# Pairs of kv tiles summed by accumulating transfers ahead of the pooling matmuls

## The chip, the cores and the metric

The kernel runs on one core of a Trainium2 chip. The metric is the device time of one execution in microseconds (us); lower is better. The median of three runs of the kernel before is 1297.57 us (1297.37 to 1297.65).

## The reference, cut to what matters

Three stages follow each other. Attention with keys and values that are pooled 4 x 4 and projected, then a gated MLP (GELU by sigmoid), then a second gated MLP (hard swish):

```python
kv_pool = kv.reshape(B, H // 4, 4, W // 4, 4, C).mean(axis=(2, 4))
k = v = kv_pool.reshape(B, -1, C) @ w_sr            # 768 keys, C = 128
a = softmax(q @ k.T / sqrt(C))                      # q: 12288 rows
x = a @ v
h = x @ moe_w_in;  x = (h * sigmoid(1.702 * h)) @ moe_w_out        # d_ff = 2048
h = x @ moe2_w_in; x = (h * clip(h + 3, 0, 6) / 6) @ moe2_w_out
```

Everything is float32. The change is in the first two lines: how the sixteen elements of each pooling window come to be summed.

## The kernel before, in words

**Tiles.** The launch code lays kv out as 3 groups of 256 keys by 4 tiles. A kv tile (`kvs`) is 128 channels by 1024 columns, 512 KB: four window elements of the 256 keys of a group. Twelve tiles come in by twelve plain loads on SyncE's queue (L578), in the order of the string `LOADS`, in which `k` is the next kv tile, `w` a 512 KB weight block (raw 64-bit words, L210) and `q` the first q tile (256 KB, L178).

**Pooling by TensorE.** `pool_mm(i)` (L590) multiplies tile i by `w_sr` in four matmuls of 256 columns, all accumulating into one PSUM tile of the group, so that the matmul does the projection and the sum of the window at once. The profile lists each float32 matmul of the program as two records. Before the first of them, `WARM` matmuls on the identity run (L561). The end of a group frees `k_hi` (L602, ScalarE), `k_lo` (L607, VectorE) and `k_copy` (L614); the last group's k is what the first score matmuls (L291) wait for.

**The head.** The string `HEAD` writes out, by hand, the order of everything up to the first two finished attention tiles: `K.i` pools tile i, `kh.g`, `kl.g`, `kf.g`, `V.g` make keys and values of group g, `Q` splits a q tile, `S`, `M`, `E`, `N` are scores, maximum, exponential and norm, `T`, `H`, `L` turn the exponentials round, `A`, `X` multiply by the values. `w.a`, `w.m`, `w.b`, `w.c`, `w.h`, `w.d` are the six steps by which VectorE and ScalarE turn one raw weight block into two float32 parts (L232 to L262). An engine takes its own instructions in this order; what stands for different engines in between matters only by the waits.

**After the head** come units of the MLPs: unit s writes 2 x 128 hidden rows (`unit_mm`), and three units later its output matmuls. `ORDER` gives the order of the pieces beside a unit, `W_STEPS` in which unit the remaining weight steps run, `T_STEPS_0` and `NORM_STEPS` where the third and fourth attention tile are turned and normed.

**Queues.** SyncE's queue issues loads in program order. A transfer that takes the place of one eight transfers back (the one load on ScalarE's queue counted in) waits until that one has landed, so that issue times tell landing times.

Of the kernel before, what the change touches and what calls it, by code (L numbers as in the profile page):

```python
# [11 lines left out]
F32 = mybir.dt.float32  # L12
# [3 lines left out]
ALU = mybir.AluOpType  # L16
AX = mybir.AxisListType

P = 128
# [18 lines left out]
H_STEPS = (6, 7, 8), (14, 16, 17)  # L38
AV_STEPS = (10, 10), (18, 18)
S_STEPS = (16, 18, 20, 22), (24, 26, 28, 30)  # L40
NORM_STEPS = 12, 12
T_STEPS_0 = {2: (3, 5, 8, 11), 3: (15, 17, 19, 21)}
V_STEPS_0 = {4: (40, 41, 42, 43), 5: (51, 51, 52, 52)}
D_STEPS_0 = {4: 44, 5: 53}
H_STEPS_0 = {4: (48, 49, 50), 5: (58, 59, 60)}
# [5 lines left out]
POOL_LO = 49, 51, 53, 57, 59  # L51

ORDER = {
    0: "v t_hi h_hi gelu t_lo w_hi w_hi_0 d hi w_0 rest hi_last h_lo w lo lo_last end".split(),
    1: "t_hi t_lo gelu hi_last hi h_hi lo_last lo v h_lo d end rest".split(),
    2: "table max w_hi_0 relu swish hi_last exp h_hi w_hi w_0 lo_last norm v h_lo d end rest w".split(),
    3: "hi_last relu lo_last swish end".split(),
}


LOADS = "k k k k w k k w k k k w k k q k w w"
HEAD = (
# [9 lines left out]
).split()  # L72


WARM = 10
W_SLOTS = 0, 1, 2, 3, 4, 3, 4, 3, 3
W_NEXT = 0, 0, 0, 1, 1, 1, 0, 1, 1, 1, 1, 0
D_POOL = (8, 11)
W_POOL = ()
W_STEPS = (  # L80
# [5 lines left out]
)  # L86
TOGETHER = 1

# [6 lines left out]
def tile_pooled_attention__moe_gelu__moe_hardswish(  # L95
# [16 lines left out]
    nc = tc.nc  # L112
    C, N = qT.shape
# [11 lines left out]
    ps_acc = ctx.enter_context(tc.tile_pool(name="ps_acc", bufs=2, space=bass.MemoryType.PSUM))  # L125
# [3 lines left out]
    ident = tiny.tile([P, P + 48], F32, name="ident", bufs=1)[:, :P]  # L129
# [3 lines left out]
    v_h = const.tile([P, KC, C], F32R, name="v_h")  # L133
    v_l = const.tile([P, KC, C], F32R, name="v_l")
# [21 lines left out]
    def f(ap):  # L156
        return ap.bitcast(F32)
# [4 lines left out]
    def act_hi(hi, x):  # L162
        nc.scalar.activation(hi, x, AF.Copy)  # L163

    def dve_lo(lo, x, hi):
        nc.vector.tensor_tensor(out=lo, in0=x, in1=f(hi), op=ALU.subtract)  # L166
# [102 lines left out]
    h = NK // 2  # L269
# [183 lines left out]

    for t, steps in T_STEPS_0.items():
        for i, step in enumerate(steps):
            at(step, "first", t_mm, t, i)
            at(step, "t_hi", t_hi, t, i)
            at(step, "t_lo", t_lo, t, i)
    for k, step in enumerate(NORM_STEPS):
        at(step, "rest", s_norm, FOUR - 1, 2 * k + 1, 2)  # L460
# [6 lines left out]
    for k in range(FOUR, NT, 2):  # L467
        s0 = 2 * k * NU
        for i in range(2):
            if k + 2 + i < NT:  # L470
                v, hh, av = ([s0 + x for x in y[i]] for y in (V_STEPS, H_STEPS, AV_STEPS))
# [84 lines left out]
    with tc.manual_schedule():  # L556
        make_identity(nc, ident)
        nc.scalar.dma_start(out=wsr_sb, in_=w_sr)
        warm = big()
        for _ in range(WARM):  # L560
            nc.tensor.matmul(warm[:, 0, :P], ident, ident, start=True, stop=True)  # L561

        n_g, n_w, kw = kvT.shape[1:]
        kg = NK // n_g
        banks = [("h", 2), ("h", 2), ("st", 1)]
        kvs, pk, kf = [], {}, {}
        for i in range(n_g * n_w):
            if i in (0, 3):
                kv3 = work.tile([P, 3, kw], F32, tag="eTl" if i else "eTh", name="kvs", bufs=1)
            if i < 6:  # L570
                kvs.append(kv3[:, i % 3, :])
            else:
                kvs.append(work.tile([P, kw], F32, tag="gl" if i % 2 else "gh", name="kvs", bufs=3))
        kv = 0
        for what in LOADS.split():
            if what == "k":
                g, w = divmod(kv, n_w)
                nc.sync.dma_start(out=kvs[kv], in_=kvT[:, g, w, :])  # L578
                kv += 1
            elif what == "w":  # L580
                w_load()
            else:
                load_q(0)

        def pool_mm(i):
            g, w = divmod(i, n_w)
            if w == 0:
                pk[g] = big(*banks[g])[:, 0, :kg]
            for c in range(kw // kg):
                nc.tensor.matmul(  # L590
                    pk[g], wsr_sb, kvs[i][:, c * kg:(c + 1) * kg],
                    start=(w == 0 and c == 0), stop=(w == n_w - 1 and c == kw // kg - 1),
                )

        def keys(g):
            cc = slice(g * kg // P, (g + 1) * kg // P)
            kh, kl = (by_quarter(a)[:, cc] for a in (k_h, k_l))
            return kh, kl, pk[g].rearrange("p (c q j) -> p c q j", q=4, j=32)

        def k_hi(g):  # L600
            kh, _, pq = keys(g)
            nc.scalar.activation(kh, pq, AF.Copy, scale=scale / (R * R))  # L602

        def k_lo(g):
            kh, kl, pq = keys(g)
            for c in range(kg // P):
                nc.vector.scalar_tensor_tensor(  # L607
                    out=kl[:, c], in0=pq[:, c], scalar=scale / (R * R), in1=f(kh)[:, c],
                    op0=ALU.mult, op1=ALU.subtract,
                )  # L610

        def k_copy(g):
            kf[g] = work.tile([P, kg], F32, tag="x2" + "hhl"[g], name="kf")
            nc.scalar.activation(kf[g], pk[g], AF.Copy, scale=1.0 / (R * R))  # L614

        def v_group(g):
            pv = ps_acc.tile([P, kg // P, C], F32, tag="acc", name="pv")
            for c in range(kg // P):
                nc.tensor.transpose(pv[:, c, :], kf[g][:, c * P:(c + 1) * P], ident)
            cs = slice(g * kg // P, (g + 1) * kg // P)  # L620
            act_hi(v_h[:, cs, :], pv)
            dve_lo(v_l[:, cs, :], pv, v_h[:, cs, :])

        def score(t, i):
            banks.append(banks.pop(0))
            s_mm(t, i, *banks[-1])

        def turn(t, i):
            banks.append(banks.pop(0))
            t_mm(t, i, *banks[-1])  # L630

        pieces = {
            "K": pool_mm, "kh": k_hi, "kl": k_lo, "kf": k_copy, "V": v_group, "Q": split_q,
            "S": score, "M": s_max, "E": s_exp, "N": s_norm, "T": turn, "H": t_hi, "L": t_lo,
            "A": lambda t: av_mm(t, range(KC)), "X": av_end, "w": w_step,
        }
        for word in HEAD:
            name, *args = word.split(".")
            pieces[name](*(int(x) if x.isdigit() else x for x in args))

        nu = len(units)
        for s in range(nu + LAG):
            run(s, "first")
            if s < nu:
                unit_mm(s)
            if s >= LAG:
                unit_out(s - LAG)
            run(s, "mm")
            m = units[s][0] if s < nu else 0
            m_last = units[s - 1][0] if 0 < s <= nu else 0  # L650
            steps = {}
            if m == 1:
                steps |= {"gelu": (unit_gelu, s), "hi": (unit_hi, s), "lo": (unit_lo, s)}
            if m == 2:
                steps |= {"relu": (unit_relu, s), "swish": (unit_swish, s)}
            if m_last == 2:
                steps |= {"hi_last": (unit_hi, s - 1), "lo_last": (unit_lo, s - 1)}
            if s >= LAG:
                steps["end"] = unit_end, s - LAG
            for place in ORDER[0 if s < FOUR * NU else 3 if s == nu - 1 else m or 2]:  # L660
                if place in steps:
                    fn, u = steps[place]
                    fn(u)
                run(s, place)
# [41 lines left out]
```

## Time and profile before

| | us |
|---|---|
| median of three runs | 1297.57 |
| the profiled execution, its own time | 1297.63 |
| its span, first to last instruction | 1295.9 |
| TensorE (PE) busy | 1288.0 (99%) |
| VectorE (DVE) busy | 1025.5 (79%) |
| ScalarE (ACT) busy | 1007.7 (78%) |
| GpSimd (POOL) busy | 173.4 (13%) |

The span leaves 1.7 us of the execution outside it. Busy shares are means over the whole span; the head is its first 66 us or so, and there the engines and the transfers are loaded quite differently from the rest. [...]

### The profile page before, as it was taken

Reading aid. Unit: us, or ns where it says so; the run is one execution under the profiler, and the core shown is the slowest. Engines: PE = TensorE matmul, PEld = TensorE weight load, DVE = VectorE, ACT = ScalarE, POOL = GpSimd, SP = SyncE. Lnnn points to the kernel's source line nnn. Section 1 sums busy time; section 2 is a strip of 40 time slices with the busy share of each in tenths; the row PEclk is TensorE's granted clock in tenths of the full one; section 3 lists DMA queues with packets and bytes.
Section 4 is the critical chain, followed back from the end, with each engine's and each line's share of the span. In section 5 each row is a group of like instructions: output and inputs, shape, how many; then the busy total and the mean of one; then the engine's idle time right before and its main releaser. Section 6 shows DMA issues by size and latency. Waiting matters only on the chain.

```text
span 1295.9 us, 16082 instructions
## 1 busy us (share of the span) xinstructions
PE 1288.0 (99%) x5834; PEld 1080.6 (83%) x5834; DVE 1025.5 (79%) x1038; ACT 1007.7 (78%) x1189; POOL 173.4 (13%) x133
## 2 busy tenths in 40 slices
PE   9999999999999999999999999999999999999998
PEld 8888888888888888888888888888888888888887
DVE  5898999986887788788688688688778868868567
ACT  2797778788788778778778878877877877877876
POOL 1402023420120021011011011002001101100000
PEclk9999999999999999999999999999999999999999
DMA  7112202203003002202201200400300220220000
GB/s 302 33 33 66 74 9 71 69 20 95 9 9 100 17 14 65 50 17 57 58 17 44 72 9 18 105 9 9 91 25 17 57 58 9 57 49 9 9 1 17
DMA packets 26527, 59.84 MB, mean 46 GB/s; under 512 B 6352, under 2 KB 6480, under 8 KB 26448
## 3 DMA queue, kind: packets, MB, share of 16 engines
q1 hardware_dynamic: 26304, 58.75, 16.1%
q8 instruction: 46, 0.75, 0.3%
q14 instruction: 33, 0.27, 0.1%
q10 hardware_dynamic: 144, 0.07, 0.0%
HBM read 21.04 MB, written 6.29 MB: 21 GB/s over the span
## 4 chain that ended last, share of the span: by engine, by line
PE 99%; ACT 1%; DVE 0%; issue 0%; POOL 0%; POOLq 0%; DVEq 0%; ACTq 0%
PE acc L540 13%; PE acc L541 13%; PE h L495 13%; PE h L494 13%; PE acc L539 13%; PE h L493 13%; PE acc L394 7%; PE st L291 7%; PE h L590 1%; PE h L291 1%; PE st L590 1%; PE st L338 0%; PE st L561 0%; PE st L394 0%; ACT eTh L163 0%; PE h L338 0%
## 5 line engine op out<-in xcount | busy, mean ns | idle before, releaser
L166 DVE TENSOR_TENSOR gl<-slots,gh 128x1024 fp32r<-128x1024 f32 (+1 forms) x380 | 469.4, 1238 | 137.5 <-ACT gh L163 137.0
L163 ACT ACTIVATE gh<-slots 128x1024 fp32r<-128x1024 f32 x385 | 405.5, 1056 | 19.8 <-PE acc L540 14.8
L540 PE MATMUL acc<-gh,w_h 128*128 128x512 f32 x768 | 299.2, 390 | 0.0
L541 PE MATMUL acc<-gl,w_h 128*128 128x512 f32 x768 | 299.1, 390 | 0.0
L539 PE MATMUL acc<-gh,w_l 128*128 128x512 f32 x768 | 298.9, 389 | 0.0
L507 ACT ACTIVATE slots<-h 128x1024 f32<-128x1024 f32 (+1 forms) x193 | 197.1, 1022 | 128.3 <-PE h L495 128.3
L513 DVE SCALAR_TENSOR_TENSOR slots<-slots,h 128x1024 f32<-128x1024 f32 (+1 forms) x193 | 234.0, 1213 | 70.1 <-ACT slots L507 68.2
L499 ACT ACTIVATE slots<-h 128x1024 f32<-128x1024 f32 x192 | 196.0, 1021 | 36.8 <-PE h L495 36.5
L540 PEld LDWEIGHTS acc<-gh,w_h 128*128 128x128 f32 x768 | 144.2, 188 | 31.0
L539 PEld LDWEIGHTS acc<-gh,w_l 128*128 128x128 f32 x768 | 144.2, 188 | 30.6
L541 PEld LDWEIGHTS acc<-gl,w_h 128*128 128x128 f32 x768 | 144.2, 188 | 30.1
L330 POOL TENSOR_SCALAR e<-e,rec 128x768 f32<-128x768 f32 x96 | 117.6, 1244 | 299.0 <-issue 173.6
L493 PE MATMUL h<-x1h,w_l 128*128 128x512 f32 x384 | 150.3, 391 | 0.3 <-ACT slots L499 0.3
L495 PE MATMUL h<-x1l,w_h 128*128 128x512 f32 x384 | 149.5, 389 | 0.0
L494 PE MATMUL h<-x1h,w_h 128*128 128x512 f32 x384 | 149.4, 389 | 0.0
L495 PE MATMUL h<-x2l,w_h 128*128 128x512 f32 x352 | 138.0, 392 | 0.0
L494 PE MATMUL h<-x2h,w_h 128*128 128x512 f32 x352 | 137.7, 391 | 0.0
L493 PE MATMUL h<-x2h,w_l 128*128 128x512 f32 x352 | 136.9, 389 | 0.0
L169 POOL TENSOR_TENSOR q_l<-q_f,q_h 128x512 fp32r<-128x512 f32 x24 | 37.4, 1556 | 598.6 <-ACT q_h L163 578.7
L493 PEld LDWEIGHTS h<-x1h,w_l 128*128 128x128 f32 x384 | 72.1, 188 | 15.5 <-ACT slots L499 0.7
L495 PEld LDWEIGHTS h<-x1l,w_h 128*128 128x128 f32 x384 | 72.1, 188 | 15.0
L313 ACT ACTIVATE e<-st,nm 128x768 f32<-128x768 f32 x86 | 77.0, 895 | 9.6 <-DVE nm L298 9.0
(99 smaller groups left out, 1453.1 us busy)
## 6 DMA issues: line engine op xcount, KB each, us to landing
eTl<-e SPq DMA_DIRECT2D x320, 96.0 KB, 2.1
kvs<-kvT SPq DMA_DIRECT2D x12, 512.0 KB, 9.4
q_f<-qT SPq DMA_DIRECT2D x24, 256.0 KB, 2.6
outT<-o SPq DMA_DIRECT2D x24, 256.0 KB, 2.0
slots<-w_in SPq DMA_DIRECT2D x8, 512.0 KB, 4.9
slots<-w_out SPq DMA_DIRECT2D x8, 512.0 KB, 4.1
wsr_sb<-w_sr ACTq DMA_DIRECT2D x1, 64.0 KB, 4.2
```

The lines of the kernel that those rows point to most:

```text
L163: nc.scalar.activation(hi, x, AF.Copy)
L166: nc.vector.tensor_tensor(out=lo, in0=x, in1=f(hi), op=ALU.subtract)
L330: nc.gpsimd.tensor_scalar(out=e, in0=e, scalar1=rec[:, r:r + 1], scalar2=1.0, op0=ALU.mult, op1=ALU.mult)
L493: nc.tensor.matmul(hp[:, c, :], wl, xh, start=True, stop=False)
L494: nc.tensor.matmul(hp[:, c, :], wh, xh, start=False, stop=False)
L495: nc.tensor.matmul(hp[:, c, :], wh, xl, start=False, stop=True)
L499: nc.scalar.activation(g, h_t.pop(u), AF.Gelu_apprx_sigmoid)
L507: nc.scalar.activation(r[:, c], h_t[u][:, c], AF.Relu, bias=3.0)
L513: nc.vector.scalar_tensor_tensor(out=g[:, c], in0=r[:, c], scalar=6.0, in1=hp[:, c], op0=ALU.min, op1=ALU.mult)
L539: nc.tensor.matmul(acc, wl, gh[:, c, :], start=first, stop=False)
L540: nc.tensor.matmul(acc, wh, gh[:, c, :], start=False, stop=False)
L541: nc.tensor.matmul(acc, wh, gl[:, c, :], start=False, stop=last)
```

## The change

Tiles 1, 3, 5, 7, 9 and 11 are no longer loaded into buffers of their own. Each is read from memory by a transfer that adds it to its even neighbour's buffer (`accum_op=ALU.add`), issued from GpSimd's queue. `pool_mm` runs for the even tiles only. Its first and last tile of a group are now taken from `HEAD`.

```diff
-NORM_STEPS = 12, 12
-T_STEPS_0 = {2: (3, 5, 8, 11), 3: (15, 17, 19, 21)}
+NORM_STEPS = 7, 12
+T_STEPS_0 = {2: (3, 6, 10, 12), 3: (15, 17, 19, 21)}
...
-LOADS = "k k k k w k k w k k k w k k q k w w"
+LOADS = "w k k w k k k k w k k k k k k q w w"
 HEAD = (
-    "w.a K.0 K.1 w.m K.2 w.b w.c w.a w.h K.3 kf.0 K.4 kh.0 w.m w.d K.5 K.6 K.7 w.b kl.0 w.h kh.1 "
-    "w.c K.8 w.a w.d w.m w.b Q.0 w.c K.9 K.10 kl.1 K.11 w.h kf.1 w.d w.a kh.2 kl.2 V.0 Q.1 kf.2 "
...
+    "w.a K.0 w.m w.b w.a w.m w.b w.c w.h w.d w.c K.2 kh.0 w.h kl.0 K.4 w.d "
+    "kf.0 K.6 w.a w.m Q.0 V.0 w.b K.8 kh.1 K.10 w.c kl.1 v.0 w.h w.d "
+    "kf.1 kh.2 Q.1 kl.2 w.a w.m S.0.0 M.0.0 S.0.1 M.0.1 kf.2 S.1.0 E.0.0 E.0.1 M.1.0 N.0.0.1 "
...
-WARM = 10
+ADDED = 1, 3, 5, 7, 9, 11
+WARM = 14
...
-D_POOL = (8, 11)
+D_POOL = (3, 5, 11)
...
             if what == "k":
                 g, w = divmod(kv, n_w)
-                nc.sync.dma_start(out=kvs[kv], in_=kvT[:, g, w, :])
+                if kv in ADDED:
+                    nc.gpsimd.dma_start(out=kvs[kv - 1], in_=kvT[:, g, w, :], accum_op=ALU.add)
+                else:
+                    nc.sync.dma_start(out=kvs[kv], in_=kvT[:, g, w, :])
                 kv += 1
...
         def pool_mm(i):
-            g, w = divmod(i, n_w)
-            if w == 0:
+            g = i // n_w
+            group = [k for k in pooled if k // n_w == g]
+            if i == group[0]:
                 pk[g] = big(*banks[g])[:, 0, :kg]
-            for c in range(kw // kg):
+            parts = kvs[i].shape[1] // kg
+            for c in range(parts):
                 nc.tensor.matmul(
                     pk[g], wsr_sb, kvs[i][:, c * kg:(c + 1) * kg],
-                    start=(w == 0 and c == 0), stop=(w == n_w - 1 and c == kw // kg - 1),
+                    start=(i == group[0] and c == 0), stop=(i == group[-1] and c == parts - 1),
                 )
```

`v_group` is cut into `v_turn` (`V`) and `v_split` (`v`), which stand apart in `HEAD`; two further pieces, `D` and `J`, are defined and not used. `W_STEPS` and the `ORDER` of stage 0 are rewritten as well.

SyncE's queue at the start of the program, before (`kvs` is a kv tile, `slots` a raw weight block; DMAHW is the completion counter of an earlier transfer):

```order
L578 DMA kvs<-kvT 128x1024 x4
L210 DMA slots<-w_in 128x1024
L578 DMA kvs<-kvT 128x1024 x2
L210 DMA slots<-w_out 128x1024 [waits DMAHW0_49]
L578 DMA kvs<-kvT 128x1024 [waits DMAHW1_49]
L578 DMA kvs<-kvT 128x1024 [waits DMAHW2_49]
L578 DMA kvs<-kvT 128x1024 [waits DMAHW3_49]
L210 DMA slots<-w_in 128x1024 [waits DMAHW4_49]
L578 DMA kvs<-kvT 128x1024 [waits DMAHW5_49]
L578 DMA kvs<-kvT 128x1024 [waits DMAHW6_49]
L178 DMA q_f<-qT 128x512 [waits DMAHW7_49]
L578 DMA kvs<-kvT 128x1024 [waits DMAHW0_49]
```

The same queue now, up to the second weight block after the last kv tile:

```order
L211 DMA slots<-w_in 128x1024
L582 DMA kvs<-kvT 128x1024
L211 DMA slots<-w_out 128x1024
L582 DMA kvs<-kvT 128x1024 x2
L211 DMA slots<-w_in 128x1024
L582 DMA kvs<-kvT 128x1024
L582 DMA kvs<-kvT 128x1024 [waits DMAHW0_49]
L582 DMA kvs<-kvT 128x1024 [waits DMAHW1_49]
L179 DMA q_f<-qT 128x512 [waits DMAHW2_49]
L211 DMA slots<-w_out 128x1024 [waits DMAHW3_49]
L211 DMA slots<-w_in 128x1024 [waits DMAHW4_49]
```

Twelve kv loads have become six, the first weight block stands ahead of the first kv tile, and still three weight blocks stand ahead of the last kv tile on this queue.

GpSimd's queue after it has made the identity, before (`q_l` is the low part of a q tile):

```order
masks.py:199 AFFINE_SELECT ident<-ident 128x128 [waits Pool_49]
L169 TENSOR_TENSOR q_l<-q_f,q_h 128x512 [waits DMAHW7_49,Activation_49]
L169 TENSOR_TENSOR q_l<-q_f,q_h 128x512 [waits DMAHW3_49,Activation_49]
L330 TENSOR_SCALAR e<-e,rec 128x768 [waits DVE_49,Activation_49] x3
L330 TENSOR_SCALAR e<-e,rec 128x768 [waits Activation_49]
```

The same place now; each L580 waits for the load of the even tile that it adds to:

```order
masks.py:199 AFFINE_SELECT ident<-ident 128x128 [waits Pool_49]
L580 DMA kvs<-kvT 128x1024 [waits DMAHW2_49]
L580 DMA kvs<-kvT 128x1024 [waits DMAHW4_49]
L580 DMA kvs<-kvT 128x1024 [waits DMAHW5_49]
L580 DMA kvs<-kvT 128x1024 [waits DMAHW7_49]
L580 DMA kvs<-kvT 128x1024 [waits DMAHW0_49]
L580 DMA kvs<-kvT 128x1024 [waits DMAHW1_49]
L170 TENSOR_TENSOR q_l<-q_f,q_h 128x512 [waits DMAHW2_49,Activation_49]
```

Six waiting issues now stand ahead of the first q split on that queue. On TensorE, these rows are the pooling now (DMASW is the completion counter of an accumulating transfer):

```order
L562 MATMUL st<-ident 128x128 x13
L608 MATMUL h<-kvs,wsr_sb 128x256 [waits DMAHW0_49,DMASW0_49]
L608 MATMUL h<-kvs,wsr_sb 128x256 x3
L608 MATMUL h<-kvs,wsr_sb 128x256 [waits DMASW1_49]
L608 MATMUL h<-kvs,wsr_sb 128x256 x3
L608 MATMUL h<-kvs,wsr_sb 128x256 [waits DMASW2_49]
L608 MATMUL h<-kvs,wsr_sb 128x256 x3
L608 MATMUL h<-kvs,wsr_sb 128x256 [waits DMASW3_49]
L608 MATMUL h<-kvs,wsr_sb 128x256 x3
```

Two more tiles follow in the same way, 24 matmuls in all where there were 48, and each of the six tiles waits for an accumulating transfer.

## Rows read from the trace of the kernel before

**Rows 1.** The page: busy time of each engine, and 40 slices of the span

```profile
PE 1288.0 (99%) x5834; PEld 1080.6 (83%) x5834; DVE 1025.5 (79%) x1038; ACT 1007.7 (78%) x1189; POOL 173.4 (13%) x133
...
PEclk9999999999999999999999999999999999999999
DMA  7112202203003002202201200400300220220000
```

**Rows 2.** Waits of PE, whole span: total us, times, longest

```profile
PE st L561 <- POOL ident masks.py:199: 1.4, 1, 1.4
PE h L338 <- DVE eTl L166: 0.7, 1, 0.7
PE st L338 <- ACT e L313: 0.6, 1, 0.6
PE st L291 <- ACT e L313: 0.5, 1, 0.5
PE h L338 <- POOL e L330: 0.4, 1, 0.4
PE h L493 <- ACT slots L499: 0.3, 1, 0.3
PE h L291 <- ACT k_h L602: 0.3, 1, 0.3
```

**Rows 3.** Windows: length, busy us by engine, PEclk, DMA share, GB/s

```profile
0.00:27.00 27.00, 25.64 (x118) 22.91 (x118) 14.70 (x29) 5.24 (x10) 2.44 (x7) 1.00 0.92 353
27.00:66.00 39.00, 36.19 (x198) 31.05 (x198) 32.04 (x59) 28.69 (x54) 14.76 (x15) 1.00 0.12 34
66.00:130.00 64.00, 64.00 (x306) 53.13 (x307) 58.34 (x77) 53.85 (x60) 8.96 (x5) 1.00 0.16 50
130.00:400.00 270.00, 270.00 (x1220) 227.06 (x1219) 234.65 (x226) 213.88 (x255) 54.63 (x36) 1.00 0.18 47
400.00:700.00 300.00, 300.00 (x1352) 251.99 (x1351) 233.31 (x225) 237.70 (x282) 39.71 (x30) 1.00 0.15 38
700.00:1296.00 596.00, 592.16 (x2648) 494.48 (x2646) 452.50 (x426) 468.37 (x533) 52.89 (x40) 1.00 0.14 36
```

**Rows 4.** Timeline of PE, first 28 us: start, us, line, count

```profile
1.36 4.63 PE L561 MATMUL st<-ident 128*128 128x128 f32 x20 [1.36 <-POOL ident masks.py:199]
5.79 14.15 PE L590 MATMUL h<-kvs,wsr_sb 128*128 128x256 f32 x64
19.77 7.07 PE L590 MATMUL st<-kvs,wsr_sb 128*128 128x256 f32 x32
26.68 0.38 PE L619 MATMUL pv<-ident,kf 128*128 128x128 f32 x2
27.32 0.61 PE L291 MATMUL h<-k_h,q_h 128*128 128x384 f32 x2 [0.26 <-ACT k_h L602]
```

**Rows 5.** Timeline of SyncE's queue: issue of the loads

```profile
8.65 0.33 SPq L210 DMA_DIRECT2D slots<-w_in  x1
9.86 1.58 SPq L578 DMA_DIRECT2D kvs<-kvT  x2
12.65 0.33 SPq L178 DMA_DIRECT2D q_f<-qT  x1
13.89 0.33 SPq L578 DMA_DIRECT2D kvs<-kvT  x1
15.09 0.33 SPq L210 DMA_DIRECT2D slots<-w_out  x1
16.34 0.33 SPq L210 DMA_DIRECT2D slots<-w_in  x1
```

**Rows 6.** Windows of 5 us in the pooling, columns as in rows 3

```profile
10.00:15.00 5.00, 5.00 (x25) 4.41 (x24) 4.03 (x9) 1.29 (x3) 0.00 (x0) 1.00 1.02 401
20.00:25.00 5.00, 5.00 (x25) 4.41 (x24) 4.83 (x10) 1.89 (x4) 1.74 (x1) 1.00 1.03 415
```

**Rows 7.** Timeline at 204 us: sixteen transfers of 96 KB within the chip

```profile
204.01 11.12 SPq L367 DMA_DIRECT2D eTl<-e  x16
```

**Rows 8.** Groups on POOL and DVE before 60 us

```profile
L169 POOL TENSOR_TENSOR q_l<-q_f,q_h 128x512 fp32r<-128x512 f32 x4 | 5.8, 1443 | 25.4 <-ACT q_h L163 25.4
L232 DVE TENSOR_SCALAR w_a<-slots 128x512 uint32<-128x512 uint32 x5 | 2.1, 424 | 11.0 <-DMA slots<-w_in 10.2 <-DMA slots<-w_out 0.8
```

More of the change, by code (lines that the diff above doesn't have):

```diff
@@ L53 @@
 ORDER = {
-    0: "v t_hi h_hi gelu t_lo w_hi w_hi_0 d hi w_0 rest hi_last h_lo w lo lo_last end".split(),
+    0: "t_hi t_lo gelu w_hi w_hi_0 hi_last h_hi h_lo hi v lo_last d w_0 w lo end rest".split(),
     1: "t_hi t_lo gelu hi_last hi h_hi lo_last lo v h_lo d end rest".split(),
@@ L583, in tile_pooled_attention__moe_gelu__moe_hardswish, with add_halves, add_next @@
                 load_q(0)
+        heads = [word.split(".") for word in HEAD]
+        pooled = [int(word[1]) for word in heads if word[0] == "K"]
+        def add_halves(i):
+            half = kvs[i].shape[1] // 2
+            near, far = kvs[i][:, :half], kvs[i][:, half:]
+            nc.vector.tensor_tensor(out=near, in0=near, in1=far, op=ALU.add)
+            kvs[i] = near
+        def add_next(i):
+            nc.vector.tensor_tensor(out=kvs[i], in0=kvs[i], in1=kvs[i + 1], op=ALU.add)
         def pool_mm(i):
-            g, w = divmod(i, n_w)
-            if w == 0:
+            g = i // n_w
+            group = [k for k in pooled if k // n_w == g]
+            if i == group[0]:
                 pk[g] = big(*banks[g])[:, 0, :kg]
-            for c in range(kw // kg):
+            parts = kvs[i].shape[1] // kg
+            for c in range(parts):
                 nc.tensor.matmul(
                     pk[g], wsr_sb, kvs[i][:, c * kg:(c + 1) * kg],
-                    start=(w == 0 and c == 0), stop=(w == n_w - 1 and c == kw // kg - 1),
+                    start=(i == group[0] and c == 0), stop=(i == group[-1] and c == parts - 1),
                 )
@@ L614, in k_copy, with v_turn, v_split @@
             nc.scalar.activation(kf[g], pk[g], AF.Copy, scale=1.0 / (R * R))
-        def v_group(g):
-            pv = ps_acc.tile([P, kg // P, C], F32, tag="acc", name="pv")
+        pv = {}
+        def v_turn(g):
+            pv[g] = ps_acc.tile([P, kg // P, C], F32, tag="acc", name="pv")
             for c in range(kg // P):
-                nc.tensor.transpose(pv[:, c, :], kf[g][:, c * P:(c + 1) * P], ident)
+                nc.tensor.transpose(pv[g][:, c, :], kf[g][:, c * P:(c + 1) * P], ident)
+        def v_split(g):
             cs = slice(g * kg // P, (g + 1) * kg // P)
-            act_hi(v_h[:, cs, :], pv)
-            dve_lo(v_l[:, cs, :], pv, v_h[:, cs, :])
+            act_hi(v_h[:, cs, :], pv[g])
+            dve_lo(v_l[:, cs, :], pv[g], v_h[:, cs, :])
         def score(t, i):
@@ L632, in tile_pooled_attention__moe_gelu__moe_hardswish @@
         pieces = {
-            "K": pool_mm, "kh": k_hi, "kl": k_lo, "kf": k_copy, "V": v_group, "Q": split_q,
+            "K": pool_mm, "kh": k_hi, "kl": k_lo, "kf": k_copy, "V": v_turn, "v": v_split, "D": add_halves, "J": add_next, "Q": split_q,
             "S": score, "M": s_max, "E": s_exp, "N": s_norm, "T": turn, "H": t_hi, "L": t_lo,
@@ L636, in tile_pooled_attention__moe_gelu__moe_hardswish @@
         }
-        for word in HEAD:
-            name, *args = word.split(".")
+        for name, *args in heads:
             pieces[name](*(int(x) if x.isdigit() else x for x in args))
```

23 rows, old and new, of tables (HEAD, W_STEPS) are left out of this document.

## The prediction

> **What bounds the kernel now.** I read the shares of the page first: PE is busy 99% of the span at a full granted clock in every slice [rows 1], so the kernel as a whole ends when TensorE has done its matmuls. The waits say the same: PE waits 4.2 us in all [rows 2]. The windows then show where there is anything to win. From 66 us to 700 us PE has no idle time at all, and the 3.8 us that it lacks after 700 [rows 3] are the last unit's drain, which the change does not touch. So nothing that happens beside the units can make the program shorter, and a microsecond that the head gains or loses goes through to the end one for one. Ahead of 66 us, PE is idle 1.4 us before 27 us, all of it before the first warm-up matmul, and 2.8 us between 27 and 66 us [rows 3].
>
> The pooling looks like pure TensorE time too: the matmuls of L590 run from 5.79 to 26.84 us without a gap [rows 4], 21.05 us for twelve tiles, 1.75 us a tile. But the transfers are full in the same stretch: DMA share 1.02 and 1.03 at 401 and 415 GB/s [rows 6]. So I asked when the last tile lands. SyncE issues a load once the one eight back has landed, so its issue times are landing times. The weight load at 8.65 us waited for kv tile 3, the one at 16.34 for kv tile 7 [rows 5]; between these two, six transfers of 512 KB landed (a weight block, tiles 4 and 5, a weight block, tiles 6 and 7): 7.69 / 6 = 1.28 us each, 410 GB/s as the windows say [rows 6]. Tile 3 is the fourth transfer, so the stream is as if it had begun at 8.65 - 4 x 1.28 = 3.53 us. Tile 11 stands behind twelve kv tiles (itself among them), three weight blocks and half a block of q: 3.53 + 15.5 x 1.28 = 23.4 us. TensorE starts on it at 26.84 - 1.75 = 25.1. **TensorE is only 1.7 us behind the transfers.** Two resources of nearly equal length lie beside each other, and the change takes work from the one and gives it to the other.
>
> **The change, part by part.**
>
> Matmuls removed: 24 of 48, 24 x 0.44 = 10.5 us of TensorE. Had TensorE alone set the end, that would be the gain. With no pooling work at all in the way, the last tile still lands at 23.4 and needs its own 1.75 us: 25.15 against 26.84, so at most 1.7 us of the 10.5 can be had unless the order of the transfers changes.
>
> Transfers: the same 6.3 MB of kv come from memory. Six come on SyncE's queue as before. Six are accumulating transfers, and no row shows one. From below: an accumulating transfer costs the engines what a plain load costs, 1.28 us. From above: besides the load it moves the tile once within the chip; the nearest row of that kind is the sixteen 96 KB transfers at 204 us [rows 7], 11.12 / 16 = 0.70 us for 96 KB, so 3.7 us for 512 KB, and 5.0 us together. I take 2.56 us: the engine must take in two tiles of 512 KB, one from memory and one from the buffer, and the nearest row to that is the plain load taken twice. The transfers of [rows 7] are cut far smaller, which is why I stay away from the upper end.
>
> [...]
>
> The sum, with everything through the same engines at a full share: ahead of the last pooled pair stand nine transfers on SyncE's queue (three weight blocks, six kv tiles), 11.5 us, and six accumulating ones, 15.4 us: 3.53 + 11.5 + 15.4 = 30.4 us. Behind them on SyncE's queue stand q and two weight blocks, 2.5 transfers or 3.2 us, which share the engines with the last additions: between 30.4 and 33.6 us. GpSimd's adds wait for their even tile, but while they wait SyncE's queue keeps the engines busy, so that waiting adds nothing to the sum. Then 1.75 us of matmuls: pooling ends at 32.2 to 35.4 us against 26.84, **5.3 to 8.5 us later**. I take 7.0, since SyncE's tail can be issued early and mostly gets through before the last addition. By the ends of the price, 1.28 and 5.0 us, pooling ends 2.4 us earlier to 0.8 later, and 20 to 23 us later.
>
> Warm-up: four more matmuls of 0.46 us (4.63 us for ten [rows 4]) end at 7.8 us. Tile 0 cannot be ready before: it is the second transfer (3.53 + 2.56 = 6.1), its addition comes after it. Cost nothing; without that cover 1.9 us.
>
> GpSimd's queue: the first q split now stands behind six waiting issues. It can start once tile 10 has landed and the last addition is issued; it takes 1.4 us [rows 8] and is needed when that addition has landed and 1.75 us of matmuls are done. Covered by a transfer of 2.56 us; if the additions are cheap, up to 1 us shows.
>
> VectorE: the first weight block is first in the queue, so its steps start near 5 us; before, VectorE waited 9.9 of the 10.2 us in the group of L232 for it [rows 8]. That is 5 us of lead on an engine which is not on the path before 27 us. From 66 to 130 us it is busy 58.3 of 64 us [rows 3] while PE has no wait, so the lead buys nothing there; if a weight came late there it would cost, but the longer head gives it more time, not less.
>
> The rewritten order from 27 to 66 us: PE's idle 2.8 us could go or double. I take zero and keep -2.8 to +2.8 for the range. `T_STEPS_0`, `NORM_STEPS`, `W_STEPS`, `D_POOL`: they lie beside a PE without idle time, so they can only cost; zero.
>
> The profiled execution took 1297.63 us, 0.06 over the median. 1297.63 + 7.0 = **1304.6 us**.
>
> **The rivals.**
>
> *The addition is as cheap as a load* (the mechanism on the other side). If the buffer is read beside the stream from memory, a tile costs 1.28 us and pooling ends 2.4 us earlier to 0.8 us later: 1297 us. For it: the bytes from memory are the same. Against: the engines are at a full share with plain loads alone [rows 6]. It decides where 9.85 us less the tail's share is left for six additions, at a price of 1.1 to 1.6 us each.
>
> *Cheap additions and an order that loses the waits.* The same, and the 2.8 us of PE idle between 27 and 66 us [rows 3] go as well, as VectorE has its lead there: about -3.6 us, 1294 us. It is the only way I find to a clear gain, since the 10.5 us of matmuls lie behind the transfers.
>
> [...]
>
> *The addition is dearer than two loads*, between 2.56 and the 5.0 us from [rows 7]: at 3.75 us, pooling ends about 15 us later, 1313 us.
>
> **How the numbers follow.** Forecast 0.38 (own range 1301.5 to 1307.5, the sum's 5.3 to 8.5 with half of the 2.8 us either way), clock 0.13, dear additions 0.09: slower, 0.60. Cheap additions 0.23: within 0.2%, which is 2.6 us and about what a measurement of this kernel can tell from no change. Cheap with the waits gone 0.17: faster. The range goes from 1294.5, which leaves out about half of the last case, to 1311, which leaves out most of the dear one and the end of the clock's.
>
> **What would show it.** Right: L608 in six bursts of eight records with PE waiting for `kvs` transfers between them; DMA share near 1 until past 30 us; pooling's last matmul at 32 to 36 us; the first L292 matmul right behind it; from there the same distance to the end as before. The price itself: the spacing of the additions' landings when SyncE's queue is empty. Wrong: the last pooling matmul before 28 us; PE's waits for transfers under 3 us in all; a PEclk below 9 in the first slice would show the clock's case. If the pooling ends late and the total does not follow, my claim that the head goes through one for one is false.

## The result and the profile after

The changed kernel takes 1307.4 us (median of three runs, 1307.35 to 1307.55) against 1297.57: ratio 1.0076, 95% interval 1.0053 to 1.0099. It is 9.8 us slower; 7.0 were forecast.

The page of the profile after, with busy times, clock, DMA shares by slice and the queues. It answers to [rows 1]:

```profile
PE 1283.0 (98%) x5794; PEld 1074.2 (82%) x5794; DVE 1025.7 (79%) x1035; ACT 1007.9 (77%) x1189; POOL 177.4 (14%) x140
...
PEclk8999999999999999999999999999999999999999
DMA  9111102203002102202200300400310220220000
```

The change shows at the start: TensorE is busy 5 us less in all, in the first slice the clock granted to TensorE (PEclk, in tenths of the full clock on the page and as a share of it in the windows) was not granted in full (8 in that slice, 0.87 in the mean of the first 38 us), and the transfers are busy for longer there. The windows, cut so that the last four answer to those of [rows 3] ten microseconds later (length, then busy us by engine, PEclk, DMA share, GB/s):

```profile
0.00:38.00 38.00, 22.20 (x85) 17.66 (x86) 15.69 (x33) 6.57 (x13) 8.26 (x14) 0.87 0.88 250
38.00:76.00 38.00, 34.81 (x192) 30.05 (x191) 32.61 (x57) 27.37 (x50) 15.23 (x16) 1.00 0.12 36
76.00:140.00 64.00, 64.00 (x307) 53.12 (x306) 58.28 (x74) 53.31 (x59) 7.47 (x5) 1.00 0.16 50
...
410.00:710.00 300.00, 300.00 (x1352) 251.99 (x1351) 233.08 (x225) 237.86 (x282) 39.65 (x30) 1.00 0.15 38
```

From 76 to 710 us TensorE has no idle time, as before from 66 to 700, and from there to the end it is idle 4.0 us where it was 3.8. The loss lies ahead of 76 us. TensorE's timeline in the pooling (start, us, line; in brackets the idle time ahead and what ended it), against [rows 4]:

```profile
1.36 6.28 PE L562 MATMUL st<-ident 128*128 128x128 f32 x28 [1.36 <-POOL ident masks.py:199]
15.94 6.49 PE L608 MATMUL h<-kvs,wsr_sb 128*128 128x256 f32 x16 [8.30 <-DMA kvs<-kvT]
23.37 1.99 PE L608 MATMUL h<-kvs,wsr_sb 128*128 128x256 f32 x8 [0.94 <-DMA kvs<-kvT]
26.82 1.99 PE L608 MATMUL h<-kvs,wsr_sb 128*128 128x256 f32 x8 [1.46 <-DMA kvs<-kvT]
28.65 0.38 PE L639 MATMUL pv<-ident,kf 128*128 128x128 f32 x2
30.66 1.97 PE L608 MATMUL st<-kvs,wsr_sb 128*128 128x256 f32 x8 [1.63 <-DMA kvs<-kvT]
34.18 1.99 PE L608 MATMUL st<-kvs,wsr_sb 128*128 128x256 f32 x8 [1.55 <-DMA kvs<-kvT]
36.65 0.62 PE L292 MATMUL h<-k_h,q_h 128*128 128x384 f32 x2 [0.47 <-ACT k_h L620]
```

Where there was one gapless row of matmuls there are now five bursts, one of sixteen records (two tiles) and four of eight, each behind a wait for a transfer. The prediction had named six bursts. The last ends at 36.17 us against 26.84: 9.3 of the 9.8 us. The first score matmul starts 9.3 us later than before. The remaining 0.5 us comes in the score stretch, as it is called here: from the first score matmul to the first GELU it was 37.46 us before (27.32 to 64.78) and is 37.94 now (36.65 to 74.59).

Two stretches of the pooling after, with the columns of the windows above:

```profile
10.00:20.00 10.00, 3.97 (x9) 2.71 (x10) 3.08 (x6) 0.00 (x0) 2.03 (x3) 0.54 1.05 276
20.00:34.00 14.00, 8.60 (x34) 6.33 (x34) 7.05 (x15) 3.37 (x8) 3.15 (x3) 0.96 1.05 268
```

The transfer engines are as full as in [rows 6], but they move 268 to 276 GB/s where they moved 401 to 415. The queues over the first 36 us (packets, MB, share of the 16 engines' time; q1 is SyncE's queue, q0 GpSimd's):

```profile
q1 hardware_dynamic: 1872, 6.29, 48.0%
q0 software_dynamic: 864, 3.15, 43.9%
```

The six additions took 0.439 x 36 = 15.8 us of all sixteen engines, 2.63 us each.

### The profile page after: what moved, and what is told of

It is laid out like the page before. It is cut to its first block, busy times and chain, and to the rows that moved or that the text cites. A ratio compares the mean times of both kernels' runs of the same rounds, so it can differ in the third digit from the quotient of the medians.

```text
span 1305.6 us, 16014 instructions
## 1 busy us (share of the span) xinstructions
PE 1283.0 (98%) x5794; PEld 1074.2 (82%) x5794; DVE 1025.7 (79%) x1035; ACT 1007.9 (77%) x1189; POOL 177.4 (14%) x140
## 4 chain that ended last, share of the span: by engine, by line
PE 96%; DMA 3%; ACT 1%; DVE 1%; issue 0%; SPq 0%; DVEq 0%; ACTq 0%
PE acc L541 13%; PE acc L542 13%; PE h L496 13%; PE acc L540 13%; PE h L495 13%; PE h L494 13%; PE acc L395 7%; PE st L292 7%; DMA kvs<-kvT 2%; PE st L339 0%; PE h L292 0%; DMA wsr_sb<-w_sr 0%; PE st L395 0%; DVE nm L299 0%; ACT e L314 0%
## 5 line engine op out<-in xcount | busy, mean ns | idle before, releaser
L495 PEld LDWEIGHTS h<-x1h,w_h 128*128 128x128 f32 x384 | 72.1, 188 | 14.7
## 6 DMA issues: line engine op xcount, KB each, us to landing
kvs<-kvT SPq DMA_DIRECT2D x6, 512.0 KB, 10.4
```

The lines of the kernel that those rows point to most:

```text
L495: nc.tensor.matmul(hp[:, c, :], wh, xh, start=False, stop=False)
```

## The experiments

Two theories to begin with. **A:** an addition occupies the transfer engines for two loads, and everything adds up to a longer stream. **B:** the way is slow and not the work: GpSimd's queue waits for each even tile, issues in 0.9 us and lands late. Every time stands beside runs of the kernel before on the same chip, 1297.73, 1297.48 and 1297.44 us in the three batches.

**The same transfers without the add**

```diff
-nc.gpsimd.dma_start(out=kvs[kv - 1], in_=kvT[:, g, w, :], accum_op=ALU.add)
+nc.gpsimd.dma_start(out=kvs[kv - 1], in_=kvT[:, g, w, :])
```

> The changed kernel with the six transfers of GpSimd's queue as plain loads: same queue, same waits for the even tile, same order everywhere, but the odd tile overwrites the even one and is not added to it, so the even tiles' share of the keys is left out. Theory A (an addition occupies the transfer engines for two loads, 2.6 us, and that alone makes the head long): six additions less 6 x 1.3 us, so the pooling's last matmul ends near 28 us instead of 36.2 and the time is 1299 us, within 1297 to 1300.5. Rival B (GpSimd's queue is the cause: waits for the even tile, slow issue of about 0.9 us, a landing that comes late): nothing changes, 1306 to 1308 us. Between 1301 and 1305: both have a share.

1299.59 us, ratio 1.0014 (1.0005 to 1.0023): theory A. Of the 9.8 us 1.9 are left, each against its own runs of the kernel before: 8.0 go with the add alone, 1.3 us for each of the six, while queue, waits and order stay. The same queue's row over the first 36 us:

```profile
q0 software_dynamic: 864, 3.15, 21.4%
```

The same packets and bytes take 7.7 us instead of 15.8, 1.28 us a tile, which is what a load on SyncE's queue took before. **The price of an addition is 2.05 loads.**

**The rewritten order alone**

```diff
-ADDED = 1, 3, 5, 7, 9, 11
+ADDED = ()
-    "w.a K.0 w.m ... K.2 kh.0 w.h kl.0 K.4 w.d "
+    "w.a K.0 K.1 w.m ... K.2 K.3 kh.0 w.h kl.0 K.4 K.5 w.d "
...
```

> The changed kernel with no tile added: all twelve tiles are loaded plainly from SyncE's queue and pooled by TensorE, each odd tile right behind its even one, and everything else of the change (order of loads, rewritten head, fourteen warm-up matmuls, steps beside the units) stays. Theory A: transfers are over by 23 us and TensorE is the bound again; it begins after fourteen warm-ups at 7.6 us, twelve tiles of 1.75 us end at 28.7, 1.8 us after the kernel before; with the 0.4 us that the score stretch has become longer the time is 1299.8 us, within 1298.5 to 1301. Rival C (the rewritten order is what costs): 1304 us or more. If the order is better than the old one behind the pooling: below 1298.

1299.07 us, ratio 1.0011 (1.0001 to 1.0020), as theory A said: by itself the order costs 1.3 us and not 9.8. TensorE in that run, which is bound by itself again and starts and ends about 1 us later than in [rows 4]:

```profile
6.88 13.98 PE L608 MATMUL h<-kvs,wsr_sb 128*128 128x256 f32 x64
20.69 0.38 PE L639 MATMUL pv<-ident,kf 128*128 128x128 f32 x2
20.91 7.07 PE L608 MATMUL st<-kvs,wsr_sb 128*128 128x256 f32 x32
```

Its score stretch is 37.97 us long (28.45 to 66.42), so the 0.5 us there belong to the rewritten order. The trace of the change shows where: a weight step on VectorE (L237), which stands ahead of the first row maximum, starts beside GpSimd's second q split, which began 0.3 us before it, and takes 1.40 us; TensorE then waits 0.61 us for the exponential behind it:

```profile
37.19 1.41 POOL L170 TENSOR_TENSOR q_l<-q_f,q_h 128x512 fp32r<-128x512 f32 x1 [7.58 <-ACT q_h L164]
37.48 1.40 DVE L237 TENSOR_SCALAR w_a<-w_a 128x512 f32<-128x512 f32 x1
40.83 0.62 PE L292 MATMUL h<-k_h,q_h 128*128 128x384 f32 x2 [0.61 <-ACT e L314]
```

In the next run below (the tail behind the additions) the split starts after the step, which takes 0.43 us, and TensorE has no such wait:

```profile
34.76 0.43 DVE L237 TENSOR_SCALAR w_a<-w_a 128x512 f32<-128x512 f32 x1
35.21 1.29 POOL L170 TENSOR_TENSOR q_l<-q_f,q_h 128x512 fp32r<-128x512 f32 x1 [6.78 <-ACT q_h L164]
```

So it is in every run of the changed order: in eight, with the change itself, the step takes 1.4 to 1.5 us and the wait 0.6 to 0.7; in the two where the split starts after the step, it takes 0.43 us and the wait is not there.

**The tail behind the additions**

```diff
-LOADS = "w k k w k k k k w k k k k k k q w w"
+LOADS = "w k k w k k k k w k k k k k k q W W"     # W: w_load on GpSimd's queue
...
```

> The changed kernel with the two weight blocks behind the last kv tile moved from SyncE's queue to GpSimd's, behind the six additions, so that they no longer share the engines with them. Theory A (all transfers add up): the additions end two loads earlier, 2.6 us, pooling ends near 33.6 us and the time is 1304.9 us, within 1304 to 1306. Rival D (the additions run at a pace of their own, each after the other, whatever else the engines do): no change, 1307 to 1308.

1304.27 us, ratio 1.0050 (1.0034 to 1.0067): theory A; the additions have no pace of their own. The last pooling burst starts at 31.46 instead of 34.18, 2.7 us earlier for two loads of 1.28. Another 0.6 us are in the score stretch, 37.34 us (33.92 to 71.26) for 37.94: the wait of 0.61 us is not there. The last three bursts each wait for a sum, so their starts tell when the sums land:

```profile
26.53 1.99 PE L610 MATMUL h<-kvs,wsr_sb 128*128 128x256 f32 x8 [1.01 <-DMA kvs<-kvT]
...
29.05 1.97 PE L610 MATMUL st<-kvs,wsr_sb 128*128 128x256 f32 x8 [0.30 <-DMA kvs<-kvT]
31.46 1.99 PE L610 MATMUL st<-kvs,wsr_sb 128*128 128x256 f32 x8 [0.44 <-DMA kvs<-kvT]
```

They are 2.5 and 2.4 us apart, which is the price read by the sign that the prediction had named. From 26 to 28 us this run shows the engines with additions and nothing else:

```profile
26.00:27.00 1.00, 0.47 (x2) 0.44 (x3) 0.93 (x3) 0.63 (x1) 0.00 (x0) 1.00 1.07 213
27.00:28.00 1.00, 1.00 (x7) 0.87 (x6) 0.96 (x2) 0.00 (x0) 0.95 (x1) 1.00 1.07 213
```

A full share at 213 GB/s, where plain loads reached 401 to 415: 1.9 loads by this reading, so that the price lies between 1.9 and 2.05.

**Half of TensorE's pooling for nothing**

```diff
-    "w.a K.0 K.1 w.m K.2 w.b w.c w.a w.h K.3 kf.0 K.4 kh.0 w.m w.d K.5 K.6 K.7 ...
+    "w.a K.1 w.m w.b w.c w.a w.h K.3 kf.0 kh.0 w.m w.d K.5 K.7 ...
...
```

> The kernel before with the matmuls of the even kv tiles left out: all twelve tiles are loaded as before, but only the odd ones enter the keys and values. It is the same saving of TensorE work as in the change (24 matmuls, 10.5 us) at no price for the transfers. Step of the prediction: the last tile lands at 23.4 us in any case, so at most 1.7 us can be had: pooling ends near 25.3 us and the time is 1296.1 us, within 1295.7 to 1297.2. Rival (TensorE is the bound of the head): about 1287 to 1290 us.

1296.68 us against 1297.48, ratio 0.9993 (0.9984 to 1.0002), inside what was expected. The same 24 matmuls saved at no price for the transfers bring 0.8 us, if anything. TensorE's last two bursts there:

```profile
20.63 2.17 PE L590 MATMUL st<-kvs,wsr_sb 128*128 128x256 f32 x8 [0.29 <-DMA kvs<-kvT]
23.68 1.99 PE L590 MATMUL st<-kvs,wsr_sb 128*128 128x256 f32 x8 [0.88 <-DMA kvs<-kvT]
```

The last tile is there at 23.68; the prediction had worked out 23.4 from the issue times. That is the floor under this head with this order of loads.

**Three additions**

```diff
-ADDED = 1, 3, 5, 7, 9, 11
+ADDED = 3, 7, 11                # K.1, K.5 and K.9 stand in HEAD again
...
```

> The changed kernel with three additions instead of six (tiles 3, 7 and 11, one for each group of keys); tiles 1, 5 and 9 are loaded plainly from SyncE's queue and pooled by TensorE. Theory A, with 1.28 us for a load and 2.6 us for an addition: 3.5 + 12 x 1.28 + 3 x 2.6 = 26.7 us for the last landing, up to 30.5 if q, the two weight blocks and the second q tile get through before it, then 2 us: pooling ends at 29 to 32.5 and the time is 1300 to 1303.5 us, nearer to the upper end. Rival B (a fixed delay of GpSimd's queue, as long as one addition ends the pooling): 1306 or more.

1306.13 us, ratio 1.0063 (1.0048 to 1.0078): outside theory A's range and just inside B's. TensorE shows why neither fits:

```profile
6.63 3.62 PE L608 MATMUL h<-kvs,wsr_sb 128*128 128x256 f32 x16
19.92 8.55 PE L608 MATMUL h<-kvs,wsr_sb 128*128 128x256 f32 x32 [9.67 <-DMA kvs<-kvT]
28.31 0.38 PE L639 MATMUL pv<-ident,kf 128*128 128x128 f32 x2
28.53 5.35 PE L608 MATMUL st<-kvs,wsr_sb 128*128 128x256 f32 x24
```

It pools tiles 0 and 1, waits 9.7 us for the first sum, and then has seven tiles left, which it works through without a gap to 33.9 us. Tiles 4 and 5 had landed by 11.40 and 12.65 us, when the loads that wait for them are issued, and were pooled behind the first sum all the same, from 19.92 us on. The sum over the transfers does not see that TensorE takes its matmuls in order. Theory G (TensorE's order is the bound here) was tried against B in two steps.

**Three additions, tail behind them** (the `W W` of above)

> Three additions (tiles 3, 7, 11), with the two weight blocks behind the last kv tile moved behind the additions on GpSimd's queue. In the run with three additions TensorE stood still from 10.2 to 19.9 us for the first sum, though tiles 4 and 5 had landed, and then worked through seven tiles without a gap to 33.9 us. Theory G (TensorE's own order is the bound there, as the matmuls behind the first sum cannot pass it): freeing the engines of 2.6 us for the last addition changes nothing, 1305 to 1306.3 us. Rival B (the last addition ends the pooling): 2.6 us less, 1303 to 1304.

1305.98 us, ratio 1.0064 (1.0050 to 1.0077): no change, as G said.

**And tiles 4 and 5 pooled ahead of the first sum**

```diff
-... w.c K.2 kh.0 w.h kl.0 K.4 K.5 w.d "
+... w.c K.4 K.5 K.2 kh.0 w.h kl.0 w.d "
```

> As the run before (three additions, weight blocks behind them), and TensorE pools tiles 4 and 5 ahead of the first sum (tiles 2 and 3). Theory G: two tiles of 1.75 us go into the wait; from 19.9 us five tiles are left, one of them perhaps at the lower clock: pooling ends at 29 to 31 us, as do the additions by 1.28 us a load and 2.6 us an addition plus the last matmuls, and the time is 1302.5 us, within 1301 to 1303.5. Rival B: as the run before, 1305 to 1306.

1305.47 us, ratio 1.0058 (1.0044 to 1.0072): a miss, only 0.5 us less, and by the time alone what rival B said.

```profile
11.33 3.72 PE L610 MATMUL h<-kvs,wsr_sb 128*128 128x256 f32 x16 [1.17 <-DMA kvs<-kvT]
19.86 3.78 PE L610 MATMUL h<-kvs,wsr_sb 128*128 128x256 f32 x8 [4.81 <-DMA kvs<-kvT]
24.54 3.78 PE L610 MATMUL h<-kvs,wsr_sb 128*128 128x256 f32 x8 [0.89 <-DMA kvs<-kvT]
28.11 0.63 PE L641 MATMUL pv<-ident,kf 128*128 128x128 f32 x2
28.53 5.77 PE L610 MATMUL st<-kvs,wsr_sb 128*128 128x256 f32 x24
```

The two tiles did move into the wait, but the two sums behind it took 3.78 us each where a lone tile takes 1.99 at a granted clock of 1.00: the granted clock was 0.50 from 20 to 25 us, after a wait of 4.8 us. The second sum also came only at 24.5. Rival B is not the reason all the same: the third addition is issued at 24.83 and lands 6.3 us later, while TensorE works from 28.53 to 34.30 without a gap. What the clock of 0.50 cost is not settled. Of the four executions three took 1305.40 to 1305.60 us at a mean granted clock of 0.996 and one took 1303.85 at 0.999, which points to 1.6 us; but the executions of the two runs above lie 1.1 and 1.5 us apart at one and the same clock.

**The same with the waits filled**

```diff
+        def fill(n):             # f.23 ahead of K.2, f.14 ahead of K.6
+            for _ in range(n):
+                nc.tensor.matmul(warm[:, 0, :P], ident, ident, start=True, stop=True)
```

> The last run with three additions (tiles 4 and 5 pooled ahead of the first sum, weight blocks behind), with 23 identity matmuls in the wait for the first sum and 14 in that for the second, so that TensorE does not stand still. There, without them, the sums of tiles 2 and 3 and of tiles 6 and 7 were pooled in 3.78 us each at a granted clock of 0.50, the second from 24.5 us on with nothing left to wait for. Theory H (the lower clock cost that run about 2 us): the second takes 2.0 us instead of 3.8 and the three behind it 5.3 instead of 5.8, pooling ends near 32 us and the time is 1303.3 us, within 1302.7 to 1304.2. Rival (the third addition is the end anyway): 1305 to 1305.8.

1304.49 us, ratio 1.0052 (1.0035 to 1.0069): 1.0 us less, between the two ranges, and none of it is won in the pooling. The clock stayed at 1.00 and the sum of tiles 6 and 7 took 1.99 us, but then the third sum was awaited until 32.33:

```profile
25.71 1.99 PE L610 MATMUL h<-kvs,wsr_sb 128*128 128x256 f32 x8 [0.23 <-DMA kvs<-kvT]
...
32.33 1.99 PE L610 MATMUL st<-kvs,wsr_sb 128*128 128x256 f32 x8 [0.95 <-DMA kvs<-kvT]
34.79 0.62 PE L292 MATMUL h<-k_h,q_h 128*128 128x384 f32 x2 [0.47 <-ACT k_h L622]
```

The first score matmul starts at 34.79 us, and in the run before it starts at 34.78. The two profiled executions differ by 0.6 us (1304.82 and 1305.40), and that is the score stretch, 37.35 us for 37.95: the second q split again starts after L237, which takes 0.43 us here and 1.40 in the run before. So theory H was right that the bursts get shorter and wrong that the end follows; the third sum is the end here, as the rival said. Its addition is issued at 26.28, 1.5 us later than in the run before, since the load of tile 10, for which it waits, lands later; why it does is not shown. The transfers look like this from there:

```profile
26.00:27.00 1.00, 1.00 (x6) 0.87 (x6) 0.93 (x3) 0.36 (x1) 0.72 (x2) 1.00 0.02 6
27.00:28.00 1.00, 1.00 (x8) 0.85 (x7) 0.88 (x2) 0.53 (x2) 1.00 (x4) 1.00 0.13 8
28.00:29.00 1.00, 1.00 (x6) 0.90 (x5) 0.84 (x4) 1.00 (x4) 1.00 (x2) 1.00 1.05 90
```

The transfer engines are nearly empty for 1.7 us after the issue. Here rival B is right: an addition with no other on the way, and two weight blocks behind it on the queue, takes 6.0 us from issue to landing, where the engines' work is 2.63 us by the price above. With six additions the engines stay full (1.05 in both stretches of the change, and no microsecond from 5 to 34 us under 0.94), and no such gap is seen.

**Warm-ups through the first wait**

```diff
-WARM = 14
+WARM = 32                        # and 56 in the second run
```

> The changed kernel with 32 warm-up matmuls instead of 14, so that TensorE works through the wait for the first pair (7.6 to 15.9 us), after which the granted clock stood at 0.50 until 21 us. Theory E (the lower clock cost nothing, as the tiles behind it wait for their additions anyway): 1307.4 us, within 1306.9 to 1307.9, with the last pooling matmul still near 36 us. Rival F (the clock is part of the 9.8 us): faster by 1 to 3 us, 1304.5 to 1306.5.

1308.47 us, ratio 1.0084 (1.0070 to 1.0098). That is outside both ranges, and it did not test what it should: the 32 were over at 10.9 us and the clock fell to 0.66 in the mean from 15 to 20 us.

> The changed kernel with 56 warm-up matmuls. With 32 they were over at 10.9 us (64 records in 9.56 us) and the granted clock still fell before the first sum came; 24 more at the pace of the later ones, 0.21 us each, reach 16 us. Theory E (the lower clock cost nothing where every later tile waits for its addition): with the clock at 1.00 all along the time is that of 32 warm-ups or of 14, 1307 to 1308.8 us. Rival F (the clock is part of the 9.8 us): 1304.5 to 1306.5.

1308.23 us, ratio 1.0082 (1.0067 to 1.0097), with the clock at 1.00 in every window from 5 to 40 us. TensorE's first and last burst:

```profile
17.10 1.99 PE L608 MATMUL h<-kvs,wsr_sb 128*128 128x256 f32 x8 [1.39 <-DMA kvs<-kvT]
...
35.16 1.99 PE L608 MATMUL st<-kvs,wsr_sb 128*128 128x256 f32 x8 [1.51 <-DMA kvs<-kvT]
```

Pooling at a clock of 1.00 throughout gains nothing: theory E. Both runs are 0.8 to 1.1 us slower than the change, because the last sum is there at 35.0 and 35.2 us instead of 34.2. It is no more work: the two queues' rows over the first 36 us are those of the change (43.9% and 47.8 to 48.0%), and from 34.4 us on the share of the engines is 0.13 at most, so that only a few of the sixteen (0.13 x 16 = 2 in the mean) end late. Why more warm-up matmuls should delay them, no run settles.

## Why the prediction was right, point by point

*TensorE is only 1.7 us behind the transfers, so little can be had.* Right, and shown: with half the pooling matmuls taken out for nothing, the last ends at 25.67 us (23.68 + 1.99), 1.2 us earlier than in [rows 4], and the time is 0.8 us less. The other 0.5 of the 1.7 us are a last tile that is there at 23.7 instead of 23.4, and its matmuls, which take 1.99 us to their end instead of 1.75.

*An addition costs two loads.* Right: 2.63 us for 2.56. The upper end, from the small transfers of [rows 7], was far off, as was the lower one. That the engines take in two tiles for one addition was my estimate; the runs show the time and the rate (213 GB/s with additions alone where plain loads reached 401 to 415), not what makes them up. The cheap rival's 9.85 us for six additions come out as 10.1 by the prediction's own figures (26.84 - 1.75 - 3.53 - 11.5); nothing hangs on it.

*The sum.* The form was right; the term that was mis-sized is the tail of SyncE's queue. I gave it half of its 3.2 us ahead of the last addition. All of it moved by then, and most of half a transfer more: the next q tile, issued at 29.64 and landed 5.2 us later, which I had not counted. Twelve loads and six additions give 3.53 + 12 x 1.28 + 6 x 2.56 = 34.3 us for the last landing (34.7 with 2.63); TensorE starts on it at 34.18, where my 7.0 us stood for 32.1. That is 2.1 of the missing 2.8 us; 0.2 are the lone last tile, 0.5 the score stretch, to which I had given zero. The run with the tail behind the additions shows the first of them: two loads moved, the last burst 2.7 us earlier. That the waits for even tiles add nothing held: the engines' share stays at 1.05. The forecast's own range, up to 1307.5 us, only just holds the result.

*Warm-up at no cost.* Right here, as the first sum comes at 15.9. In the run without additions tile 0 lands at 6.27 us, 5.1 us after its issue, and the same fourteen matmuls hold it back to 6.88 (5.79 before).

*GpSimd's queue.* Right: the first q split ends at 29.61, the scores start at 36.65. It is the second split that costs, beside L237.

*VectorE's lead.* Right that it buys nothing beside the units: VectorE is busy 58.28 of 64 us from 76 us on, as it was from 66. But one of its weight steps, L237, stands on the path of the score stretch, which the prediction had not looked at.

*The clock.* The chance of 0.13 was my estimate, as the clock stood at 1.00 in every row of before. Its sign appeared: PEclk is 8 in the first slice. In the first wait, 8.3 us long, the granted clock fell to 0.50, where it stood from 11 to 21 us, and the two tiles pooled from 15.94 us on took 6.49 us, where two tiles took 3.72 at 1.00 (tiles 4 and 5 ahead, 11.33 us). But it was at 1.00 again from 22 us on, ahead of the last four tiles, and behind the two tiles TensorE still waited 0.94 us for the next sum, so that a clock of 1.00 throughout brings nothing: 1308.23 us with 56 warm-up matmuls. With three additions, where a tile at 0.50 had nothing left to wait for, a single execution points to 1.6 us, no more than such runs are apart.

*The head goes through one for one.* Right: 9.3 us at the first score matmul, 9.8 at the end.

## What to carry to other kernels

Before work is moved from the busiest engine to the transfers, read when the data lands: here a gapless row of matmuls ended 1.7 us behind what a full transfer queue allowed, so 10.5 us of matmuls were worth 0.8 us when they were left out. An accumulating transfer saved no transfer here; it took the engines' time of two (2.63 us for 1.28), and what was queued beside it shared in the delay: the two weight blocks behind the last kv tile landed 23.8 and 25.1 us after their issue, where it was 10.5 and 10.4 before. Here a sum over a full queue held while it stayed full (1.05 with six additions; with three and the waits filled the engines were nearly empty for 1.7 us) and while the engine behind it could take the pieces as they landed: in program order, one sum awaited for 9.7 us held back seven tiles.

## What the runs showed of the hardware that I had not expected

An accumulating transfer of 512 KB takes 2.63 us of all sixteen engines where a plain one from the same queue takes 1.28, and additions alone moved 213 GB/s (the tail behind them). Issued into nearly empty engines, with two weight blocks behind it, one (the third in the run with filled waits) moved nothing for 1.7 us and landed 6.0 us after its issue. The first addition of the change, issued at 6.65 us into a full queue (share 1.03), was usable at 15.94, 9.3 us later. TensorE's granted clock was 0.50 at the end of a wait of 8.3 us (the change), and after one of 4.8 us too (three additions, tiles 4 and 5 ahead). A VectorE step of 0.43 us took 1.40 us where it started beside a q split on GpSimd.
